# First x and w1 loads on one queue, shared tail transposes and a shifted copy on ScalarE, in a squared-ReLU MLP kernel

## The chip, the cores and the metric

The kernel runs on one core of one Trainium2 chip. The metric is the device time of one execution in microseconds (us). The profiler's span, from the first to the last instruction, is 1.7 to 2.1 us shorter than that time. A ratio is the mean time of one kernel's fast runs over the mean of the fast runs of the kernel before in the same rounds, so it is not quite the ratio of the medians quoted beside it. All landing times of single loads below come from the landing records of the traces, counted from the start of the span; a load has landed when the last of its 16 engines has reported.

## The reference, cut to what matters

```python
# x: 1 x 2048 x 576, w1: 576 x 4608, b1: 4608, w2: 4608 x 576, b2: 576, all bf16
h = jnp.einsum("bsd,df->bsf", x, w1) + b1
r = jnp.where(h > zero, h, zero)
h = r * r
out = jnp.einsum("bsf,fd->bsd", h, w2) + b2
```

The contraction length 576 is 4 x 128 + 64. The kernel works on four blocks of 512 rows of x. For the 64 rows that are left over, it runs two 64-row matmuls side by side on the two halves of the array (in the trace of the kernel before, the first two both start at 9.06 us and take 0.39 us). For that the kernel holds the transposed x (xT) twice, the second time shifted by 64 partitions.

## The kernel before

Only the start is touched by the change. TensorE runs warm-up matmuls on constants. It then transposes block 0 of x, 128 x 128 at a time, runs 32 matmuls of 256 columns for the first 512 features (`part`, h is the half of the block and k the contraction tile), then four paired 64-row matmuls (`pair`), and goes into the long dense stage on the rest of w1 (`a_rows`, tile `w_h`).

```python
WARM = [512] * 6 + [256]
...
load_x(nc.sync, 0)
load_x(nc.scalar, 1)
load_x(nc.sync, 2)
load_x(nc.scalar, 3)
for k in range(NK):                                    # NK = 4
    load_w1n(nc.sync if k % 2 == 0 else nc.scalar, k, k + 1)
...
for h in range(2):
    load_w1n8(nc.sync, h)                              # 64 rows of w1, then the w_h loads follow
...
PLACE = [(0, 0), (0, 1), (1, 0), (1, 1), (0, 2)]
T_ORDER = [0, 1, NK, 2, 3]
def x_transpose(j):
    h, q = divmod(j, 2)
    for k in T_ORDER:                                  # five transposes for each x tile
        bank, slot = PLACE[k]
        c0 = k * P if k < NK else D - P
        keep(nc.tensor.transpose(tb[h][bank][:, slot, q * P:(q + 1) * P], xs[:, j, c0:c0 + P], ident[:]))
...
for j in range(2):
    x_transpose(j)
x_copies(0)
for j in range(2, RT):
    x_transpose(j)
x_copies(1)
dup_windows(0)                                         # the two shifted copies, both on VectorE
for k in range(NK):
    part(0, k)
part(1, 0)
make_b1T()
for k in range(1, NK):
    part(1, k)
```

## Time and profile before

| | before |
|---|---|
| median before the prediction, 3 runs | 290.67 us (290.65 to 291.33) |
| TensorE busy, of span | 284.6 of 288.7 us |
| first transpose | 3.76 us |
| first 256-column matmul | 5.41 us |
| first weights of the dense stage | 9.29 us |

First the page of the kernel before: the first line gives each engine's busy time with its share of the span, the second the chain that ended last, by engine.

```profile
PE 284.6 (99%) x2027; PEld 138.9 (48%) x2032; DVE 78.6 (27%) x177; ACT 96.5 (33%) x152; POOL 0.9 (0%) x7
...
PE 97%; DMA 1%; SPq 0%; issue 0%; DVE 0%
```

TensorE bounds everything. Only a start that lets the dense stage begin sooner can save time. The timeline of TensorE in the first 9.3 us (start, duration, what, count):

```profile
0.78 2.93 PE L63 MATMUL wps<-const-bfloat16-1.0 128*128 128x512 bf16 x7 [0.78 <-PEq L328]
3.76 1.52 PE L146 MATMUL tb<-ident,x_sb 128*128 128x128 bf16 x20
5.41 2.36 PE L217 MATMUL pn<-xTw,w1n 128*128 128x256 bf16 x20
7.60 0.22 PE L159 MATMUL b1T_ps<-ident,b_rows 128*128 128x128 bf16 x1
7.66 1.47 PE L217 MATMUL pn<-xTw,w1n 128*128 128x256 bf16 x12
```

Once the first 256-column matmul runs, nothing stops the chain until the dense stage: 5.41 to 9.29 us, 3.88 us. The waits of the weight load (PEld) in the first 12 us, as total, number and longest, show what it waited for ahead of that:

```profile
PEld L146 <- DMA x_sb<-in_x_dram: 1.0, 2, 0.7
PEld L217 <- DMA w1n<-in_w_dram: 0.3, 1, 0.3
```

So the start is paced by loads: x tiles landed at 3.53, 3.72, 4.34 and 4.51 us, w1 tiles at 5.15, 5.36, 5.84 and 6.06. The windows view (stretch, length, busy time of PE, PEld, DVE, ACT and POOL with counts, granted clock, share of the 16 DMA engines, GB/s):

```profile
2.00:2.50 0.50, 0.50 (x3) 0.22 (x2) 0.00 (x0) 0.00 (x0) 0.00 (x0) 1.00 1.00 247
3.00:3.50 0.50, 0.50 (x3) 0.01 (x1) 0.00 (x0) 0.50 (x1) 0.00 (x0) 1.00 0.93 320
4.50:5.00 0.50, 0.45 (x8) 0.45 (x9) 0.50 (x3) 0.00 (x0) 0.00 (x0) 1.00 1.09 379
```

The DMA engines are full while x and w1 come in (shares of 0.93 to 1.09). The mean over the six stretches from 2 to 5 us is 318 GB/s. The clock of 1.00 in these lines is not to be trusted: the trace's first clock record says that the clock went up at 3.66 us, and where a trace has no record yet the view prints 1.00. The warm-up matmuls of 512 columns start 427 ns apart, those of 256 columns later 109 to 110 ns apart. "The clock was up at" means the time of that record from here on.

### The profile page before, as it was taken

What the parts mean: (1) busy time and instruction counts of PE and PEld (TensorE: products, weight loads), DVE (VectorE), ACT (ScalarE), POOL (GpSimd) and SP (SyncE); (2) the same over time, 40 slices, a digit from 0 to 9 for tenths busy, and PEclk for the clock granted to TensorE, in tenths of its full rate; (3) what the DMA queues carried; (4) which work ended last, traced back from release to release, by engine and by line L of the source; (5) the groups of instructions that cost most, each with busy time, mean ns of one, the idle gap of its engine ahead of it and who ended that gap; (6) DMA issues with size and microseconds to landing.
All of it is one profiled execution on the core that took longest, in us unless ns stands there. A gap on an engine that the chain in (4) does not pass through costs nothing.

```text
span 288.7 us, 4690 instructions
## 1 busy us (share of the span) xinstructions
PE 284.6 (99%) x2027; PEld 138.9 (48%) x2032; DVE 78.6 (27%) x177; ACT 96.5 (33%) x152; POOL 0.9 (0%) x7
## 2 busy tenths in 40 slices
PE   8999999999999999999999999999999999999996
PEld 5544444444444555555544444444444455555555
DVE  3444544444500200000025444444440001100001
ACT  3666666666500000000027666666670000000000
POOL 0000000000000000000000000000000000000000
PEclk9999999999999999999999999999999999999999
DMA  6999999600001100000000000000000110000000
GB/s 198 236 244 197 265 388 246 94 0 2 0 18 36 37 16 18 16 16 18 16 16 2 1 2 0 2 0 2 0 2 0 36 39 16 16 16 19 32 17 18
DMA packets 31573, 16.59 MB, mean 57 GB/s; under 512 B 15552, under 2 KB 31552, under 8 KB 31552
## 3 DMA queue, kind: packets, MB, share of 16 engines
q1 hardware_dynamic: 30928, 15.72, 22.3%
q10 hardware_dynamic: 624, 0.57, 0.7%
q8 instruction: 16, 0.26, 0.4%
q14 instruction: 5, 0.04, 0.0%
HBM read 11.43 MB, written 2.36 MB: 48 GB/s over the span
## 4 chain that ended last, share of the span: by engine, by line
PE 97%; DMA 1%; SPq 0%; issue 0%; DVE 0%
PE ph L181 42%; PE po L272 38%; PE pt L253 11%; PE pn L202 4%; DMA w1n<-in_w_dram 1%; PE pn L217 1%; PE ph L183 1%; PE pn L196 1%; SPq L72 0%; DVE o_sb L274 0%; PE b1T_ps L159 0%; PE pn L198 0%
## 5 line engine op out<-in xcount | busy, mean ns | idle before, releaser
L181 PE MATMUL ph<-xTw,w_h 64*128 64x512 bf16 x576 | 124.6, 376 | 0.0
L183 PE MATMUL ph<-xTw,w_h 64*128 64x512 bf16 x576 | 124.6, 376 | 0.0
L272 PE MATMUL po<-w_sb,hT 128*128 128x448 bf16 (+2 forms) x612 | 109.4, 341 | 0.0
L169 ACT ACTIVATE r<-ph,b1T 128x512 bf16<-128x512 f32 x128 | 81.1, 685 | 41.6 <-PE ph L183 41.6
L181 PEld LDWEIGHTS <-w_h 64*128 64x128 bf16 x576 | 54.1, 94 | 68.3
L272 PEld LDWEIGHTS <-hT 128*128 128x128 bf16 x612 | 58.5, 98 | 51.0
L170 DVE TENSOR_TENSOR hT<-r 128x512 bf16<-128x512 bf16 x144 | 61.2, 426 | 76.9 <-ACT r L169 76.9
L183 PEld LDWEIGHTS <-w_h 64*128 64x128 bf16 x576 | 54.1, 94 | 0.0
L274 DVE TENSOR_TENSOR o_sb<-po,b_bc 128x448 bf16<-128x448 f32 (+2 forms) x17 | 10.2, 597 | 125.8 <-PE po L272 125.8
L253 PE MATMUL pt<-hT,w_sb 128*128 128x512 bf16 x142 | 31.3, 379 | 0.1
L169 ACT ACTIVATE r<-pn,b1T 128x512 bf16<-128x512 f32 x16 | 10.3, 688 | 62.0 <-PE pn L198 60.6
L253 PEld LDWEIGHTS <-w_sb 128*128 128x128 bf16 x144 | 14.1, 98 | 17.0
L256 ACT ACTIVATE oT<-pt,b2T 128x512 bf16<-128x512 f32 x4 | 2.7, 687 | 28.3 <-PE pt L253 28.3
L202 PE MATMUL pn<-xTw,w1n 128*128 128x512 bf16 x45 | 10.4, 379 | 0.4 <-issue 0.3
L202 PEld LDWEIGHTS <-w1n 128*128 128x128 bf16 x48 | 4.5, 98 | 6.0 <-issue 0.8
L217 PE MATMUL pn<-xTw,w1n 128*128 128x256 bf16 x32 | 3.7, 273 | 0.1
L63 PE MATMUL wps<-const-bfloat16-1.0 128*128 128x512 bf16 (+1 forms) x7 | 2.9, 597 | 0.8 <-PEq L328 0.8
L217 PEld LDWEIGHTS <-w1n 128*128 128x128 bf16 x32 | 3.0, 98 | 0.6 <-DMA w1n<-in_w_dram 0.3
L115 DVE COPY xTw<-xTw 64x2048 bf16<-64x2048 bf16 x4 | 2.8, 690 | 0.6 <-ACT xTw L152 0.5
L116 DVE COPY xTw<-xTw 64x2048 bf16<-64x2048 bf16 x4 | 2.8, 688 | 0.1
L196 PE MATMUL pn<-xTw,w1n 64*128 64x512 bf16 x8 | 2.4, 379 | 0.0
L198 PE MATMUL pn<-xTw,w1n 64*128 64x512 bf16 x8 | 2.4, 379 | 0.0
(21 smaller groups left out, 10.5 us busy)
## 6 DMA issues: line engine op xcount, KB each, us to landing
w_sb<-in_w_dram SPq DMA_DIRECT2D x2, 2592.0 KB, 15.2
w_h<-in_w_dram SPq DMA_DIRECT2D x14, 288.0 KB, 6.6
out_dram<-o_sb SPq DMA_DIRECT2D x15, 112.0 KB, 1.7
w_h<-in_w_dram SPq DMA_DIRECT2D x4, 144.0 KB, 3.2
out_dram<-ot SPq DMA_DIRECT2D x4, 128.0 KB, 2.0
x_sb<-in_x_dram ACTq DMA_DIRECT2D x2, 144.0 KB, 3.0
x_sb<-in_x_dram SPq DMA_DIRECT2D x2, 144.0 KB, 3.0
w1n<-in_w_dram ACTq DMA_DIRECT2D x2, 128.0 KB, 3.6
```

The costliest lines, as they stand in the source:

```text
L63: keep(nc.tensor.matmul(wps[:, 0:n], lhsT=ones[:, 0:P], rhs=ones[:, 0:n], start=True, stop=True))
L115: keep(nc.vector.tensor_copy(out=xT[0:H, SPC:SPC + 4, :], in_=xT[H:P, E3:E3 + 4, :]))
L169: keep(nc.scalar.activation(out=r[:], in_=bank[:], func=ACT.Relu, bias=b1T[:, ft:ft + 1], scale=1.0))
L170: keep(nc.vector.tensor_tensor(out=hTs[sb][:, ft, :], in0=r[:], in1=r[:], op=ALU.mult))
L181: keep(nc.tensor.matmul(bx[:], lhsT=w1_h[0:H, LO_C[i], jc], rhs=xT[0:H, LO_W[i], :], start=(i == 0), stop=(i == NC - 1)))
L183: keep(nc.tensor.matmul(by[:], lhsT=w1_h[H:P, UP_C[i], jc], rhs=xT[H:P, UP_W[i], :], start=(i == 0), stop=(i == NC - 1)))
L196: keep(nc.tensor.matmul(banks[2 * i][:], lhsT=w1n8[0:H, 2 * i * P:(2 * i + 1) * P], rhs=xT[0:H, SPC, :], start=start, stop=stop, skip_grou ...
L202: keep(nc.tensor.matmul(banks[g][:], lhsT=w1n[:, k, g * P:(g + 1) * P], rhs=xT[:, O + k, :], start=start, stop=stop))
L217: keep(nc.tensor.matmul(banks[g][:, hc], lhsT=w1n[:, k, g * P:(g + 1) * P], rhs=xT[:, O + k, hc], start=(h == 0 and k == 0), stop=False, s ...
L253: keep(nc.tensor.matmul(pt[:], lhsT=w2_sb[:, ft, DM:D], rhs=hT[:, ft, :], start=(i == 0), stop=(i == NFT - 1)))
L272: keep(nc.tensor.matmul(po[:, 0:d1 - d0], lhsT=hT[:, ft, jj * P:(jj + 1) * P], rhs=w2_sb[:, ft, d0:d1], start=(i == 0), stop=(i == NFT - 1)))
L274: keep(nc.vector.tensor_tensor(out=o_sb[:, d0:d1], in0=po[:, 0:d1 - d0], in1=b2_bc[:, d0:d1], op=ALU.add))
```

## The change

Its intent is to let the first matmuls start sooner. x is to arrive first, undisturbed, on one queue. Two transposes are saved by transposing the 64 tail columns of two x tiles together (`transpose_tails`, fed by two GpSimd copies). Only what the first matmuls need is done before them. ScalarE makes one of the shifted copies, and the warm-up is 0.32 us shorter (384 of 3328 columns, at the 1.2 columns per ns of the warm-up, 512 in 427 ns). The core of the diff:

```diff
-    WARM = [512] * 6 + [256]
+    WARM = [512] * 5 + [384]
...
-    load_x(nc.sync, 0)
-    load_x(nc.scalar, 1)
-    load_x(nc.sync, 2)
-    load_x(nc.scalar, 3)
-    for k in range(NK):
-        load_w1n(nc.sync if k % 2 == 0 else nc.scalar, k, k + 1)
+    for rt in range(RT):
+        load_x(nc.sync, rt)
+    for k0, k1 in [(0, 1), (1, 2), (2, NK)]:
+        load_w1n(nc.sync, k0, k1)
...
+    xs8 = const.tile([P, RT, H], BF16, name="xs8")
+    for h in range(2):
+        keep(nc.gpsimd.tensor_copy(out=xs8[:, 2 * h:2 * h + 2, :], in_=xs[:, 2 * h:2 * h + 2, NK * P:D]))
...
-    W2CH = 18
+    W2CH = 12
...
+    def dup_windows_first():
+        keep(nc.scalar.copy(out=xT0[0:H, E:E + 3, :], in_=xT0[H:P, O:O + 3, :]))
+    def transpose_tails():
+        tl = ps_h.tile([P, 2, P], BF16, name="tl", tag="ph")
+        for h in range(2):
+            keep(nc.tensor.transpose(tl[:, h, :], xs8[:, 2 * h:2 * h + 2, :], ident[:]))
...          # four copies out of tl and two shifted copies, on VectorE
-                for j in range(2):
+                for j in range(RT):
                     x_transpose(j)                    # four transposes for each tile now
-                x_copies(0)
...
-                for k in range(NK):
-                    part(0, k)
-                part(1, 0)
-                make_b1T()
-                for k in range(1, NK):
+                dup_windows_first()
+                part(0, 0)
+                part(0, 1)
+                transpose_tails()
+                part(0, 2)
+                part(0, 3)
+                for k in range(NK):
                     part(1, k)
+                    if k == 1:
+                        make_b1T()
```

More of the change, by code (lines that the diff above doesn't have):

```diff
@@ L137 @@
     tb = [[ps_h.tile([P, 4, HS], BF16, name="tb", tag="ph") for _ in range(2)] for _ in range(2)]
-    PLACE = [(0, 0), (0, 1), (1, 0), (1, 1), (0, 2)]
-    T_ORDER = [0, 1, NK, 2, 3]
     def x_transpose(j):
         h, q = divmod(j, 2)
-        for k in T_ORDER:
-            bank, slot = PLACE[k]
-            c0 = k * P if k < NK else D - P
-            keep(nc.tensor.transpose(tb[h][bank][:, slot, q * P:(q + 1) * P], xs[:, j, c0:c0 + P], ident[:]))
-    def x_copies(h):
-        hc = slice(h * HS, (h + 1) * HS)
-        for k in (0, 1):
-            keep(nc.vector.tensor_copy(out=xT0[:, O + k, hc], in_=tb[h][0][:, k, :]))
-        keep(nc.scalar.copy(out=xT0[:, O + 2:O + 4, hc], in_=tb[h][1][:, 0:2, :]))
-        keep(nc.vector.tensor_copy(out=xT0[:, E3, hc], in_=tb[h][0][:, 2, :]))
-    b1T = const.tile([P, NFT], FP32, name="b1T")
+        hc = slice(h * HS, (h + 1) * HS)
+        for bank in range(2):
+            for k in range(2 * bank, 2 * bank + 2):
+                keep(nc.tensor.transpose(tb[h][bank][:, k % 2, q * P:(q + 1) * P], xs[:, j, k * P:(k + 1) * P], ident[:]))
+            for k in range(2 * bank, 2 * bank + 2) if q == 1 else ():
+                copy = nc.scalar.copy if h == 1 and bank == 1 else nc.vector.tensor_copy
+                keep(copy(out=xT0[:, O + k, hc], in_=tb[h][bank][:, k % 2, :]))
+    b1T = const.tile([P, NFT], FP32, name="b1T")
+    def dup_windows_first():
[4 more added lines that the diff above has]
+            keep(nc.tensor.transpose(tl[:, h, :], xs8[:, 2 * h:2 * h + 2, :], ident[:]))
+        x8 = xT0.rearrange("p c (h q t) -> p c h q t", h=2, q=2)
+        for q in range(2):
+            keep(nc.vector.tensor_copy(out=x8[H:P, E3, :, q, :], in_=tl[q * H:(q + 1) * H, 0:2, :]))
+        for q in range(2):
+            keep(nc.vector.tensor_copy(out=x8[0:H, SPC, :, q, :], in_=tl[q * H:(q + 1) * H, 0:2, :]))
+        keep(nc.vector.tensor_copy(out=xT0[H:P, SPC:SPC + 4, :], in_=xT0[0:H, O:O + 4, :]))
+        keep(nc.vector.tensor_copy(out=xT0[0:H, E3, :], in_=xT0[H:P, O + 3, :]))
     def make_b1T():
@@ L219, in part @@
                                               skip_group_check=True))
-                for j in range(2):
+                for j in range(RT):
                     x_transpose(j)
-                x_copies(0)
-                for j in range(2, RT):
-                    x_transpose(j)
-                x_copies(1)
-                dup_windows(0)
+                dup_windows_first()
[4 more added lines that the diff above has]
+                part(0, 3)
                 for k in range(NK):
-                    part(0, k)
-                part(1, 0)
-                make_b1T()
-                for k in range(1, NK):
                     part(1, k)
+                    if k == 1:
+                        make_b1T()
             else:
@@ L286 @@
     b2T = const.tile([P, 1], FP32, name="b2T")
-    nc.gpsimd.tensor_copy(out=b2T[:], in_=b2_col[:])
+    keep(nc.gpsimd.tensor_copy(out=b2T[:], in_=b2_col[:]))
     keep(nc.sync.dma_start(out=b2_bc[:], in_=b2.partition_broadcast(P)))
-    for c in range(2):
+    for c in range(3):
         load_w2(c)
```

## The prediction

> **What bounds the kernel now.** TensorE: busy 284.6 of 288.7 us (first part of the page); the chain of waits is 97% matmuls. From 9.3 us to the end it streams without gaps, and nothing critical changes there (w2 in three loads lands long before use). The whole effect lies in the first 9.3 us.
>
> Timeline of that start: warm-up matmuls from 0.78 to about 3.5 us at half speed (427 ns apart). Transposes wait for x until 3.76 (0.75 us) and again 0.23 us, end at 5.11, wait 0.29 us for the first w1 tile. From 5.40, 32 matmuls of 256 columns, 108 ns apart, run to 9.06; then the paired 64-row matmuls; the dense stage on the w1 halves loads its first weights at 9.29. Landings in the trace: x 3.53, 3.72, 4.34, 4.51; w1 tiles 5.15, 5.36, 5.84, 6.06. From 2 to 5 us the engines move 290 to 360 GB/s (windows): bandwidth, not issue.[...]
>
> **What the change does.**
> - x and w1 go in order on one queue. An issue takes 0.40 to 0.45 us for 131 to 147 KB, about 330 GB/s, so the queue just feeds the engines. Estimates: x lands at 3.0, 3.5, 3.9, 4.3; w1 k=0 at 4.6, k=1 at 5.0, k=2,3 at 5.6 to 5.8.
> - 20 transposes become 18 (0.11 us less), two of them later, so the first matmuls start about 4.7 instead of 5.40 and the 32 end near 8.4 to 8.5 instead of 9.06: 0.6 us gained.
> - ScalarE's table load (1.28 us) moves forward. Its new shifted copy of 64x1536 (estimate 1.4 us, from 588 ns for 512 columns), VectorE's tail copies (four of about 0.25 us) plus 0.69 and 0.3 us end near 7.7: hidden. GpSimd's two tail copies (about 0.3 us, from its 294 ns operation) too.
> - New cost: SyncE issues seven loads before the 64-row w1 loads (0.58 us each) and the w1 halves. Before, the first halves were issued at 4.79 and 5.49 and landed at 7.63 and 8.83, only 0.46 us before use. I expect issues at 5.0 and 5.7, the second landing at 9.0 to 9.1. TensorE reaches it at 8.7 and waits 0.3 to 0.4 us: most of the gain is given back. The dense stage starts at 9.0 (8.6 to 9.5) instead of 9.29.
>
> The shorter warm-up (2944 columns for 3328, 0.32 us) ends near 3.2, about when x arrives. If gaps delay the clock's rise, transposes run cold, mostly in time that waits for x.[...] this trace shows the rise once, before 3.76 us.
>
> **Predicted: 290.35 us**, range 289.7 to 290.9. Faster by over 2%: 0.01; within 2%: 0.98; slower by over 2%: 0.01.
>
> **What would show each step.** x landings staggered by 0.45 us, the first before 3.5; first 256-column matmul near 4.7; 64-row matmuls near 8.5; a new wait of TensorE's weight load on a w1-half DMA before the dense stage, 0.2 to 0.5 us; no wait on shifted copies or GpSimd; everything after shifted by the same amount.
>
> **What would make it wrong.** One queue slower than two; cold clock into the 256-column matmuls (up to 108 ns more each); the first w1 halves landing as early as before, which gives the full 0.6 us (near 290.0); or late bias rows, whose landing gates the second w1-half issue.

## The result

The changed kernel is slower by a third of a per cent: 291.82 us median (291.39 to 293.02, 6 runs) against 290.95 (290.65 to 291.33, 6 runs) of the kernel before, ratio 1.0034, 95% interval 1.0015 to 1.0054. It lies inside the 2% that count as the same, but outside the predicted range of 289.7 to 290.9, and on the other side of zero. The same file run again in a later batch gave 1.0038 (1.0018 to 1.0058).

The timeline of TensorE in the changed kernel, to be held against the one above:

```profile
0.78 2.61 PE L63 MATMUL wps<-const-bfloat16-1.0 128*128 128x512 bf16 x6 [0.78 <-PEq L337]
3.18 1.06 PE L145 MATMUL tb<-ident,x_sb 128*128 128x128 bf16 x8
4.70 0.87 PE L145 MATMUL tb<-ident,x_sb 128*128 128x128 bf16 x8 [0.45 <-DMA x_sb<-in_x_dram]
5.46 0.61 PE L227 MATMUL pn<-xTw,w1n 128*128 128x256 bf16 x4
6.61 0.61 PE L227 MATMUL pn<-xTw,w1n 128*128 128x256 bf16 x4 [0.54 <-DMA w1n<-in_w_dram]
7.05 0.28 PE L158 MATMUL tl<-ident,xs 128*128 128x128 bf16 x2
7.54 1.92 PE L227 MATMUL pn<-xTw,w1n 128*128 128x256 bf16 x16 [0.21 <-DMA w1n<-in_w_dram]
```

The first transposes do start sooner, 3.18 instead of 3.76 us. But the first 256-column matmul starts at 5.46, where it was at 5.41, and the chain after it, unbroken before, now has two holes. The dense stage loads its first weights at 10.55 us, 1.26 later than before; the span grew by 1.25 us (290.0 for 288.7). The waits of the weight load in the first 12 us name the cause:

```profile
PEld L227 <- DMA w1n<-in_w_dram: 1.2, 2, 0.8
PEld L145 <- DMA x_sb<-in_x_dram: 1.1, 2, 0.7
```

The wait on w1 is 0.9 us longer than before, and it now falls between matmuls. Windows of the changed kernel:

```profile
2.00:2.50 0.50, 0.50 (x3) 0.22 (x2) 0.00 (x0) 0.22 (x2) 0.00 (x0) 1.00 0.89 284
3.00:3.50 0.50, 0.50 (x5) 0.42 (x4) 0.00 (x0) 0.00 (x0) 0.01 (x1) 1.00 0.95 154
3.50:4.00 0.50, 0.50 (x7) 0.47 (x5) 0.00 (x0) 0.00 (x0) 0.28 (x1) 1.00 0.67 182
5.00:5.50 0.50, 0.50 (x8) 0.35 (x7) 0.01 (x1) 0.00 (x0) 0.29 (x1) 1.00 0.58 152
```

The DMA engines move fewer bytes while the same loads wait to be served: 256 GB/s as the mean from 2 to 5 us, where it was 318. The share in this view is to be read with care, as it counts a packet's whole time in the stretch where the packet starts. Spread over their real times, the packets of the trace keep the engines busy for 0.62 of the time from 3 to 3.5 us, 0.98 from 3.5 to 4 and 0.70 from 5 to 5.5; in the kernel before it is 1.01, 0.96 and 0.90. So from 3 to 3.5 and from 5 to 5.5 us they are partly idle. Some packets of the first of these stretches are also slow: ten took over 200 ns, the slowest 622, where the median x row takes 51 ns; in the kernel before one packet there took over 200 ns (359). The x tiles landed at 2.97, 3.35, 4.65 and 5.08 us, w1 k=0 at 5.41, k=1 at 6.56, and k=2,3, one load now, at 7.49.

The loads are also issued later. The tile view of w1n shows the issues (ns as minimum, median and maximum, then the first and last start in us) and the time from issue to landing, in which the two 64-row loads are counted too. The kernel before:

```profile
L76 ACTq DMA_DIRECT2D w1n<-in_w_dram x2: 453/454/454, 1.6 to 2.1; - x2
L76 SPq DMA_DIRECT2D w1n<-in_w_dram x2: 433/436/440, 1.7 to 2.2; - x2
DMA to landing us min/median/max: 2.5/3.6/3.9
```

The changed kernel:

```profile
L76 SPq DMA_DIRECT2D w1n<-in_w_dram x3: 432/432/434, 2.6 to 3.5; - x3
DMA to landing us min/median/max: 2.8/3.5/3.9
```

SyncE starts one issue every 0.47 us, so the last of its seven starts at 3.54 us; with two engines issuing, the last of the eight started at 2.16. From issue to landing a w1 load takes about as long as before. So the late tiles may in part be late issues; the experiments do not separate this from slower delivery.

### The profile page after: what moved, and what is told of

Same layout as the page of the kernel before. It is cut to its first block, busy times and chain, and to the rows that moved or that the text cites. A ratio compares the mean times of both kernels' runs of the same rounds, so it can differ in the third digit from the quotient of the medians.

```text
span 290.0 us, 4699 instructions
## 1 busy us (share of the span) xinstructions
PE 285.4 (98%) x2029; PEld 139.1 (48%) x2029; DVE 79.2 (27%) x181; ACT 97.4 (34%) x153; POOL 1.7 (1%) x9
## 3 DMA queue, kind: packets, MB, share of 16 engines
HBM read 11.43 MB, written 2.36 MB: 48 GB/s over the span
## 4 chain that ended last, share of the span: by engine, by line
PE 96%; DMA 1%; SPq 1%; issue 0%; DVE 0%
PE ph L191 42%; PE po L281 38%; PE pt L262 11%; PE pn L212 4%; DMA w1n<-in_w_dram 1%; PE pn L227 1%; PE ph L193 1%; PE pn L206 1%; SPq L72 1%; SPq L76 0%; DVE o_sb L283 0%; PE b1T_ps L169 0%; PE pn L208 0%
## 5 line engine op out<-in xcount | busy, mean ns | idle before, releaser
L145 PE MATMUL tb<-ident,x_sb 128*128 128x128 bf16 x16 | 1.9, 294 | 0.5 <-DMA x_sb<-in_x_dram 0.5
L148 DVE COPY xTw<-tb 128x256 bf16<-128x256 bf16 x6 | 1.4, 284 | 3.7 <-PE tb L145 3.7
```

## The experiments

Sixteen kernels ran. "B" stands for the kernel before, "A" for the changed one; each diff is against the one named.

**How fine the scale is.** `before_again` is B against itself.

> The kernel before, unchanged, against itself: a control. Ratio 1.000, and the interval shows what this comparison can tell apart. Its profile is a second sample of chance: [...] the w1 landings may differ from the first profile's 5.36 to 6.06 by some tenths. If both are fixed by the program: 3.66 and 5.4 to 6.1 again.

Measured: 1.0002, interval 0.9987 to 1.0017. So a single comparison here settles nothing below 0.0015, or 0.4 us; executions of B spread from 290.29 to 291.65 us over all batches. The second profile: w1 tiles at 5.26 to 6.32 us, clock up at 3.77 us, dense stage at 9.19.

**The changed kernel again.** `after_again` is A, unchanged.

> The changed kernel, unchanged, for a second profile and a closer ratio. Queue theory: 1.002 to 1.004, waits of 0.4 to 1.2 us on w1 tiles between the 256-column matmuls, last w1 tile landing at 7.1 to 7.5 us again (two queues: 6.1 to 7.0).

Measured: 291.81 us, ratio 1.0038. Its waits, in the same view:

```profile
PEld L145 <- DMA x_sb<-in_x_dram: 1.5, 3, 0.7
PEld L227 <- DMA w1n<-in_w_dram: 1.0, 2, 0.6
```

The last w1 load landed at 7.30 us, the dense stage began at 10.36. In this execution the clock was up at 3.67 us, as early as in B's first profile (3.66), so the loss needs no late clock. From the first 256-column matmul to the dense stage: 3.88 us in both profiles of B (5.41 to 9.29, 5.31 to 9.19), 5.09 and 4.89 in the two of A (5.46 to 10.55, 5.47 to 10.36). B's two profiles are of fast executions, 290.52 and 290.55 us of a spread of 290.29 to 291.65, and A's are near A's median, so the 1.25 us between the first two spans is somewhat more than the change costs on average (about 1.05 us).

**Which part does it?** `a_two_queues` is A with B's loads, `b_one_queue` is B with all eight loads on SyncE.

```diff
# a_two_queues, against A
-    for rt in range(RT):
-        load_x(nc.sync, rt)
-    for k0, k1 in [(0, 1), (1, 2), (2, NK)]:
-        load_w1n(nc.sync, k0, k1)
+    (the six lines of B: x and w1 alternate between nc.sync and nc.scalar)
# b_one_queue, against B
-    (the same six lines)
+    for rt in range(RT):
+        load_x(nc.sync, rt)
+    for k in range(NK):
+        load_w1n(nc.sync, k, k + 1)
```

> The changed kernel with only the loads put back as before: x and w1 tiles alternate between the SyncE and ScalarE queues, w1 in four loads. Queue theory (one queue cannot keep the 16 engines fed: 8 to 13 of them busy between 2.75 and 3.5 us and between 4.5 and 7 us, where two queues kept about 16 busy from 2.0 to 5.0): w1 k=1 lands near 5.2 and k=2,3 near 6.0 again, the pairs start at 8.8 to 9.1 instead of 10.32, time 290.3 to 291.0, ratio to before 0.998 to 1.000. Rival (the rearranged transposes, tail copies, the shifted copy on ScalarE or the shorter warm-up cost the time): still about 1.003.

> The kernel before with only the loads changed: all four x tiles and all four w1 tiles on SyncE's queue, in order; transposes, copies and warm-up as before. Queue theory: the whole loss or more, w1 k=1 lands past 6.0 and k=3 past 7.0, ratio 1.002 to 1.006. Rival (the rest of the change costs the time): ratio 1.000 within 0.001.

Measured: `a_two_queues` 291.18 us, 1.0010 (0.9997 to 1.0023); `b_one_queue` 291.30 us, 1.0013 (1.0002 to 1.0025). Giving A two queues takes away about 70% of its loss. Taking B's second queue away seems to cost something, but its 0.0013 is no more than the control can tell apart; it is less than A's whole loss. Neither theory gets all of it: in A the queue is the larger part, not the only one. In `b_one_queue` the weight loads of the 256-column matmuls and of the dense stage wait:

```profile
PEld L215 <- DMA w1n<-in_w_dram: 0.8, 2, 0.5
...
PEld L181 <- DMA w_h<-in_w_dram: 0.3, 1, 0.3
```

The second line is the wait on a w1 half that the prediction expected; in A it does not show, as TensorE comes later still.

The landings tell the queues apart better than the times. Nine profiles have w1 alternating over two queues after x (B and A alike), six have the seven or eight small loads on one queue:

| | w1 k=0 landed, mean (range) | last w1 tile landed, mean (range) |
|---|---|---|
| two queues, 9 profiles | 5.69 (5.26 to 6.25) | 6.58 (6.06 to 6.98) |
| one queue, 6 profiles | 5.67 (5.41 to 6.21) | 7.28 (7.13 to 7.49) |

One queue is no later with k=0, the tile that the first matmul needs, but 0.70 us later with the last, and the ranges do not overlap. With two queues the later tiles are mostly there before the unbroken chain asks for them; with one they are not.

**The merged load.** `a_split` is A with w1 k=2 and k=3 as two loads.

```diff
-    for k0, k1 in [(0, 1), (1, 2), (2, NK)]:
+    for k0, k1 in [(0, 1), (1, 2), (2, 3), (3, NK)]:
```

> The changed kernel, one queue, with w1 k=2 and k=3 as two loads of 128 KB in place of one of 256 KB. If the merged load is what made the matmuls of k=2 wait (it lands as a whole, at 7.49 us[...]): ratio near 1.0013, as in the kernel before on one queue. If not: about 1.0034, as the change as a whole.

Measured: 291.40 us, 1.0021 (1.0008 to 1.0033). The tiles landed at 5.58, 6.38, 6.93 and 7.28 us, so k=2 was there 0.4 to 0.6 us sooner than in A's two profiles. The direction is that of a cost of the merged load, about 0.4 us by the medians, but the intervals overlap.

**Is one queue slow in itself?** `a_one_queue_big` is A with one load for all of x and one for all of w1, both on SyncE.

```diff
-    for rt in range(RT):
-        load_x(nc.sync, rt)
-    for k0, k1 in [(0, 1), (1, 2), (2, NK)]:
-        load_w1n(nc.sync, k0, k1)
+    keep(nc.sync.dma_start(out=xs[:, :, :], in_=x2[0:SB, :].rearrange("(r p) d -> p r d", p=P)))
+    load_w1n(nc.sync, 0, NK)
```

> The changed kernel, still on SyncE's queue alone, but x as one load of 512 rows and w1 as one load of 512 rows: two issues in place of seven. If the queue starves the engines because each issue (0.46 us for 128 to 147 KB) or each boundary between loads costs time, the engines stay near 16 busy, x and w1 all land by about 5.5 and the pairs start near 9.3 or earlier; ratio about 1.000.[...]

Measured: 292.98 us, 1.0076 (1.0059 to 1.0094), much slower, but this does not show that one queue is slow in itself. Its windows:

```profile
2.50:3.00 0.50, 0.50 (x3) 0.08 (x1) 0.00 (x0) 0.00 (x0) 0.00 (x0) 1.00 0.57 145
4.00:4.50 0.50, 0.00 (x0) 0.00 (x0) 0.00 (x0) 0.00 (x0) 0.00 (x0) 1.00 1.08 383
5.00:5.50 0.50, 0.50 (x7) 0.50 (x6) 0.00 (x0) 0.00 (x0) 0.39 (x2) 1.00 1.08 385
```

After a start at half rate, one queue carries 383 to 394 GB/s from 3.5 to 5.5 us. The four w1 tiles, now one load, landed at 6.33 us, within the range of two queues and before the last tile of any run with small loads on one queue (7.13 at the earliest); SyncE had issued it by 1.74 us. So one queue did fill the engines here (a share of 1.08) once the large loads were under way; it did not at the start, nor with the small loads of A (0.62 from 3 to 3.5 us). That one queue is used is thus not enough to make w1 late. Whether the small loads are late because they are issued one after the other or because they are delivered more slowly, these runs do not say. The time is lost because x lands as a whole at 4.81 us, so TensorE stands idle from 3.4 to 4.86 us, and its clock rises only at 9.87 us.

**Order matters too.** `a_w1_on_act` is A with x on SyncE and w1 on ScalarE.

```diff
-    for k0, k1 in [(0, 1), (1, 2), (2, NK)]:
-        load_w1n(nc.sync, k0, k1)
+    for k in range(NK):
+        load_w1n(nc.scalar, k, k + 1)
```

> The changed kernel with x on SyncE's queue and the four w1 tiles on ScalarE's. Queue theory: two queues are in flight again, so the engines stay near 16 busy from 2 to 5 us; x shares with w1 and lands later (x3 past 4.5), but w1 k=3 lands near 6; SyncE is free sooner, the w1 halves are issued near 4 instead of 5.3. Time 290.0 to 291.0, ratio 0.997 to 1.000. Rival (the rest of the change): about 1.003.

Measured: 294.52 us, 1.0124 (1.0108 to 1.0139), against my expectation. Both queues were in flight and the last tile came at 6.98 us, within the range of two queues, but x now shared the engines with w1 from the start: x tiles landed at 3.35, 4.52, 5.74 and 6.77 us. TensorE's weight load waited 3.4 us for x in all, in four waits. Worse, its clock fell again. Windows of this run; the granted clock is the third number from the end:

```profile
3.90:7.30 3.40, 1.38 (x16) 0.92 (x16) 1.04 (x5) 0.27 (x3) 0.58 (x2) 1.00 0.78 230
7.30:10.70 3.40, 3.40 (x20) 2.51 (x18) 2.03 (x7) 2.06 (x3) 0.00 (x0) 0.51 0.78 182
```

In the first stretch TensorE was busy 1.38 of 3.40 us; in the next it got half its clock. The trace's clock records stand at 3.93 (up), 7.35 (down) and 10.76 us (up), 3.41 us apart both times. That the idle time brought the clock down is my reading of this one run; no other run tests it.

**The clock.** `b_half_warm` is B with `WARM = [512] * 3`, `b_short_warm` is B with A's warm-up `[512] * 5 + [384]`, `a_warm` is A with B's warm-up `[512] * 6 + [256]`.

> The kernel before with the warm-up cut to three matmuls (0.78 to 2.06 us), so that TensorE stands idle 1.7 us until the first x tile. Nothing else changes and no useful work waits for the warm-up. Clock theory:[...] the transposes and many of the 256-column matmuls run at half speed, ratio 1.003 to 1.008. Rival (holes before the first transpose do not matter): 1.000.

> The kernel before with only the warm-up shortened as in the change (2944 columns for 3328). Clock theory ([...] a hole between warm-up and first transpose makes an early rise rarer): the hole grows from 0.2 to 0.5 us,[...] ratio 1.0005 to 1.002. Rival (the warm-up's length does nothing as long as the x tiles are waited for): 1.000 within 0.0005.

> The changed kernel with only the warm-up put back to 3328 columns. Clock theory: holes of the warm-up phase shrink, ratio falls from 1.0034 to about 1.002. Queue theory alone: the time is set by the landing of w1 k=1 and k=2,3, so 1.003 to 1.004, or more since the x tiles are there at 3.0 and now wait for the warm-up until 3.5.

Measured: `b_half_warm` 291.79 us, 1.0034 (1.0016 to 1.0051), with the clock up only at 9.27 us in its profile, which is of its slowest execution (292.68 us). Its TensorE timeline:

```profile
0.78 1.44 PE L63 MATMUL wps<-const-bfloat16-1.0 128*128 128x512 bf16 x3 [0.78 <-PEq L328]
3.52 2.32 PE L146 MATMUL tb<-ident,x_sb 128*128 128x128 bf16 x20 [1.30 <-DMA x_sb<-in_x_dram]
5.80 4.03 PE L217 MATMUL pn<-xTw,w1n 128*128 128x256 bf16 x20
```

The 20 transposes took 2.32 us here and 1.52 in B, waits included, and the first 20 matmuls 4.03 us for 2.36. No useful work waits for the warm-up, yet the part of it that was cut is worth 1 us (the 1.0034), and the slower transposes and matmuls show the clock as the reason. `b_short_warm`: 291.37 us, 1.0014 (1.0002 to 1.0027), clock up at 7.12 us in its profile, again of its slowest execution. `a_warm`: 291.55 us, 1.0024 (1.0011 to 1.0036), against 1.0034 and 1.0038 with the short one. Both point the expected way by about 0.001, which is below the control's 0.0015, so a cost of the shorter warm-up is not settled.

**Does the rearrangement itself cost time?** `b_long_warm` and `a_long_warm` have `WARM = [512] * 22`, so that every x and w1 tile has landed and the clock is up before the first transpose.

> The kernel before with a warm-up of 22 matmuls of 512 columns, so that the clock is up and every x and w1 tile has landed before the first transpose: shows TensorE's own chain without clock and loads. From the first transpose to the first weight load of the dense stage: 20 transposes at 56 ns, 32 matmuls at 109 ns, one b1 transpose and the paired matmuls: about 5.2 us plus the wait for the first copies of about 0.4: 5.3 to 5.7 us.

> The same long warm-up in the changed kernel. If the change's own rearrangement costs nothing: first transpose to the dense stage 0.1 us shorter than in the kernel before with the long warm-up, or up to 0.4 us shorter, as the copies of the first half are done while the second half is transposed. Rival (the rearrangement costs time of its own, by tail transposes that wait for GpSimd, or by VectorE's longer list of copies): 0.2 us longer or more, with a wait of TensorE on a copy to show for it.

The timelines, first `b_long_warm`:

```profile
7.52 1.32 PEld L146 LDWEIGHTS <-x_sb 128*128 128x128 bf16 x20
...
12.72 0.09 PEld L181 LDWEIGHTS <-w_h 64*128 64x128 bf16 x1
```

then `a_long_warm`:

```profile
7.51 1.10 PEld L145 LDWEIGHTS <-x_sb 128*128 128x128 bf16 x16
9.39 0.21 PEld L158 LDWEIGHTS <-xs 128*128 128x128 bf16 x2
...
12.61 0.09 PEld L191 LDWEIGHTS <-w_h 64*128 64x128 bf16 x1
```

From the first transpose to the dense stage it is 5.20 us in B and 5.10 in A: with loads and clock out of the way the change is 0.10 us shorter, the two saved transposes. The tail copies on GpSimd and VectorE and the shifted copy on ScalarE make nothing wait. But in the real kernel this gain does not show. In B all 20 transposes are done before w1 k=0 lands. In A two of the 18 come after it. With two queues they lengthen the chain: from the first 256-column matmul to the dense stage, `a_two_warm2` below takes 4.00 us (5.67 to 9.67) without a hole, B 3.88. In A itself they cost nothing, as TensorE waits for w1 k=2,3 after them anyway (the 0.21 us before the matmul at 7.54, in the timeline of the result).

**What is left with two queues and the old warm-up.** `a_two_warm` and `a_two_warm2` are the same kernel, A with B's loads and B's warm-up. `a_two_warm_fill` also does the four removed transposes again, without use:

```diff
# a_two_warm_fill, against a_two_warm
         hc = slice(h * HS, (h + 1) * HS)
+        keep(nc.tensor.transpose(tb[h][0][:, 2, q * P:(q + 1) * P], xs[:, j, D - P:D], ident[:]))
```

> The changed kernel with the loads on two queues as before and the warm-up put back: only the shared tail transposes, the copies' new split over engines and the w2 chunks are left of the change. If loads and warm-up are the whole loss: ratio 0.998 to 1.000 (0.1 us fewer transposes). If the rest of the change costs something of its own: 1.001 as in the run with two queues and the short warm-up.

> The kernel of the run with two queues and the restored warm-up, once more, as the partner of the next run on the same chip: its ratio of 1.002 with one execution at 293.37 and a clock that rose only at 9.60 us is not explained by loads or by TensorE's own chain (which the long warm-up showed to be 0.1 us shorter). If it was chance: within 0.001 of 1.000. If it is real: 1.001 to 1.003 again.

> The same kernel with the four transposes that the change took out done again, one per x tile, into a part of the PSUM tile that nobody reads. Activity theory (the removed transposes leave TensorE less busy while it waits for x[...]): 0.0005 to 0.002 below its partner[...]. Rival (no such effect): the same as its partner or 0.2 us slower.

Measured: 291.59 us, 1.0020 (1.0006 to 1.0033); 291.17 us, 1.0011 (0.9997 to 1.0024); with fill 291.26 us, 1.0014 (1.0000 to 1.0028). The filler made no difference, so my idea that the missing transposes delay the clock fell. The clock was up at 9.60, 3.75 and 4.27 us in the three profiles, the first two of one kernel, so it varies between executions. The execution with 9.60 was profiled at 293.37 us, the slowest of this kernel, 1.8 us above its median. With two queues the changed kernel gave 1.0010 to 1.0020 four times. Of that, the exposed tail transposes, about 0.11 us, are 0.0004; the rest is below what these comparisons settle. The two runs with the old warm-up and no filler (1.0020 and 1.0011) are no faster than `a_two_queues` with the short one (1.0010).

**A version to beat both.** `b_interleave` is B with the loads in the order x0, x1, w1 k=0, k=1, x2, x3, k=2, k=3, alternating between the queues, and the matmuls of the first half for k=0,1 before the transposes of x2 and x3.

```diff
                 x_copies(0)
+                part(0, 0)
+                part(0, 1)
                 for j in range(2, RT):
                     x_transpose(j)
                 x_copies(1)
                 dup_windows(0)
-                for k in range(NK):
-                    part(0, k)
+                part(0, 2)
+                part(0, 3)
```

> Built from the findings: the kernel before, two queues, with the order x0 x1, w1 k=0 k=1, x2 x3, w1 k=2 k=3, and the first half's matmuls of k=0,1 placed before the transposes of x2 and x3. TensorE starts the 256-column matmuls near 4.5 us instead of 5.4 and has fewer holes, so the clock rises no later. Expected: dense stage at 8.7 to 9.0, held there by the first w1 halves that land at 8.8, ratio 0.998 to 0.9995. If loads do not pace this start at all: 1.000 or above.

Measured: 291.06 us, 1.0007 (0.9994 to 1.0019), no gain. The first 256-column matmul started at 4.94 us, but the clock was up only at 6.05 in the profile: the first eight took 1.56 us, where the first eight of `a_two_warm2`, with the clock up at 3.75, took 1.05. The dense stage began at 9.90. Whether an execution with an early clock gains was not seen.

## Why the prediction was wrong

- **Right: where the time is decided.** Only the first 10 us matter; the span grew by 1.25 us and the start of the dense stage moved by 1.26, so nothing after it, the three w2 loads included, costs time.
- **Wrong, and the step that failed: "the queue just feeds the engines."** I divided the size of a load by its issue time, got 330 GB/s, and took it as the rate of delivery. An issue took what I said (0.40 to 0.43 us in the changed kernel), but the issues start 0.47 us apart, which for 131 to 147 KB is about 280 to 315 GB/s, and the rate from 2 to 5 us was lower still, 256 GB/s. I expected w1 at 4.6, 5.0 and 5.6 to 5.8 us; it landed at 5.41, 6.56 and 7.49, in the second profile at 5.42, 6.11 and 7.30. The x tiles were expected at 3.0, 3.5, 3.9 and 4.3 and came at 2.97, 3.35, 4.65 and 5.08: right while the queue began, wrong from the third on. In place of a gain of 0.6 us at the matmuls the trace has a first matmul 0.05 us later and holes of 1.2 us after it.
- **Wrong: "bandwidth, not issue", read from full engines.** The engines were full with two queues feeding them (318 GB/s from 2 to 5 us). That view of B could not say what one queue would do with the same loads. I had listed "one queue slower than two" under what would make it wrong, without a number.
- **Wrong: what the saved transposes are worth.** 0.11 us was right for TensorE's own chain (0.10 with the long warm-ups), but nothing of it was gained: the saved ones had been hidden behind the wait for w1. The two moved ones are hidden by another wait for w1 in A, and cost 0.11 us once the loads are in time (`a_two_warm2`).
- **Right in kind, absent here: the wait on a w1 half.** It shows in B on one queue (0.3 us). In the changed kernel the first halves were in time, as TensorE was late.
- **Right: copies hidden.** The shifted copy on ScalarE took 1.47 us (estimate 1.4), GpSimd's tail copies 0.29 us each, and no wait on them shows.
- **Under-rated: the clock.** I named it as a risk (up to 108 ns more for each 256-column matmul) and expected cold transposes to fall mostly into time that waits for x. It came up 1.6 us apart in two executions of A (5.25 and 3.67) and 5.8 us apart in two of A with two queues and the old warm-up (9.60 and 3.75). `b_half_warm`, with the clock up at 9.27 us in its profile, lost about 1 us (1.0034); whether the shorter warm-up has a share in A's loss is not shown.

Where the loss is: 1.0036, the mean of the two runs of A, is 1.05 us at 290.9 us. Of that 0.64 us goes when the second queue comes back, if A is held against the mean of all four runs with two queues (1.0014; three of them have the old warm-up), or 0.76 us against `a_two_queues` alone (1.0010; the same warm-up as A). The merged load may be a part of that. Of what is left with two queues, 0.3 to 0.4 us, 0.11 us is the tail transposes, exposed by then. The rest, 0.2 to 0.3 us, is below what one comparison settles. The shorter warm-up is a candidate (`b_short_warm`, `a_warm`), but putting it back gained nothing once the loads were on two queues.

## What to carry to other kernels

A profile with full DMA engines shows that the present set of queues fills them, not that fewer would (318 GB/s from 2 to 5 us on two here, 256 on one): before taking a queue away at the start of a kernel, where loads are small (131 to 147 KB here) and their latency counts (2.8 to 3.9 us from issue to landing in the kernel before), measure on one queue when the loads are issued and when they land, and look at the last tile, not at the first. Judge a queue's pace by the time from one issue to the next (0.47 us here), not by the length of an issue (0.40 to 0.43 us). Work saved or moved on the bounding engine counts only if it lies after the last wait that remains: two transposes taken from a time that was idle anyway and put behind it are a loss (0.12 us of chain in `a_two_warm2`). Filler work before the first real matmul was not waste here: with half of it left out, `b_half_warm` had its clock up only at 9.27 us and a ratio of 1.0034. After a stretch in which TensorE was busy 1.38 of 3.40 us, `a_w1_on_act` ran 3.41 us at half clock. So judge a start by several executions and run the kernel before against itself to know what a comparison can settle.
